# Normalised linear attention and channel mix on one core: batch 0's normalisation and token mix in fewer passes, and another written order

## The chip, the cores and the metric

The kernel runs on one core of a Trainium2 chip. The metric is the device time of one execution in microseconds (us); a time of the kernel is the median over several runs. The profile is one further execution, recorded by the hardware profiler. Its engines are TensorE (PE, with its weight loads as PEld), VectorE (DVE), ScalarE (ACT), GpSimd (POOL) and SyncE (SP). POOL and SP, and once ScalarE, also issue the transfers between the chip's main memory and the on-chip memory. Each engine executes its own instructions strictly in the order in which the program issued them; a wait at the head of an engine's queue holds all that stands behind it.

## The reference, cut to what matters

```python
# attention: q, k, v are [8 batches, 8 heads, 576 tokens, 64]
kv  = einsum('bhsd,bhse->bhde', k, v)
u   = einsum('bhsd,bhde->bhse', q, kv)
x   = u / sqrt(mean(u * u, axis=-1) + 1e-6) * g_norm      # then [batch, 576, 512]
# channel mix
x_prev = x shifted by one token within each batch (zeros first)
xk = mu_k * x + (1 - mu_k) * x_prev
xr = mu_r * x + (1 - mu_r) * x_prev
kk = maximum(xk @ w_k, 0)                # w_k is [512, 1024]
out = sigmoid(xr @ w_r) * ((kk * kk) @ w_v)
```

All inputs and the output are fp32; the kernel's matmuls take bf16.

## The kernel before

Attention goes by batch (0 to 7). For batches 0 and 1 the eight heads are handled as two halves z = 0 and 1; for the later ones both halves go together, which the names show as `.01`. The channel mix goes by groups g = 0 to 8 of 512 tokens, across batch borders, so group 2 takes tokens of batches 1 and 2, group 3 of batches 2 and 3.

Every step is a named piece: `add(name, engines, function, deps, bufs)`. The string `ORDER` lists all pieces, and `emit` (line 41) issues them in that order; `@A` or `@D` behind a name chooses ScalarE or VectorE. There is no planner at run time: the string alone fixes the order on each engine and on each transfer queue. The pieces of batch b, half z (and i for one half of the tokens):

- `ld.k`, `ld.v`, `ld.q`: loads with a cast to bf16, issued by POOL (lines 221 and 226); `ld.wk`, `ld.wv`, `ld.wr`: the weights (line 252). They go through one queue in the order of their issue. k, v and q have three buffers each. `ldh.k`, `ldh.v` are fp32 loads of batch 0's first half issued by SP (line 236), and `cst` casts them.
- `kv` (line 265) forms k times v in PSUM; `kc` copies it out, `ks` (line 271) rearranges it on TensorE, `kd` copies it again. `tq` (line 349) transposes q on VectorE. `u` (line 282) is q times kv, in PSUM.
- `uc` (line 368) takes u out of PSUM, scaled with g_norm, to the bf16 tile `uT`. `sq` (line 370) squares u on ScalarE. `ss` sums the squares over a head on TensorE (line 395 for batches 0 and 1, line 379 later). `rs` makes 1/rms on ScalarE (line 288). From batch 2 on, `sp` (line 417) spreads it with eight transfers of SP.
- `mul` (line 392) multiplies uT with 1/rms into `xT`. In `blends` (line 294), `d` is x minus x_prev; `mk` and `mr` scale d with mu - 1, two instructions each; `xk` and `xr` add x (line 313).
- The mix of group g: `k` (line 494, and 469 for group 0), `relu` (452), `ksq` (480 and 509), `r` (521), `sig` (531), `v` (541), `out` (554, and 568 for the last group), `st` for the stores (443).

`perm` and `ident` are two constant tables that POOL builds after VectorE has cleared them (`setp`); `cols` holds g_norm and mu - 1 as columns; `z:512` and `zz` are matmuls of zeros, which fill TensorE until data are there. `table` loads ScalarE's table for either 1/rms or the sigmoid when the other is loaded.

PSUM has four buffers `ps` for everything. In the order before, TensorE passes kv4.01 behind ss3 and two pieces ahead of the end of group 1's `v`.

Of the kernel before, what the change touches and what calls it, by code (L numbers as in the profile page):

```python
# [10 lines left out]
ALU = mybir.AluOpType  # L11
# [1 line left out]


ORDER = """
ldh.k ldh.v ld.q0.0 small table seta setp ident ld.v0.1 ld.k0.1 ld.q0.1 ld.q1.0 ld.v1.0 ld.k1.0 perm ld.wk0 ld.wk1 ld.k1.1 ld.v1.1 ld.wv0 ld.q1.1 ld.wv1 ld.wr ld.k2.01 ld.v2.01 ld.q2.01 zz cst.k0@A cst.k1@A cst.v1@D cst.v0@A z:512 z:512 z:512 z:512 z:512 z:512 z:512 z:512 z:512 z:512 z:512 z:512 z:512 z:512 z:512 z:512 kv0.0 setb tq0.0.1 kc0.0@A z:512 z:512 ks0.0 tq0.0.0 tr9 kd0.0@D z:512 z:512 z:512 u0.0.1 sq0.01 kv0.1 ld.v3.01 ld.k3.01 cols u0.0.0 sq0.00 uc0.01@D uc0.00@A kc0.1@D z:512 z:512 z:512 ss0.00 rs0.00 z:512 ss0.01 tq0.1.0 tq0.1.1 ld.q3.01 mul0.00 ks0.1 kd0.1@A d0.00 rs0.01 z:512 z:512 u0.1.0 uc0.10@A sq0.10 u0.1.1 uc0.11@A z:512 z:512 z:512 z:512 z:512 ss0.10 mul0.01 d0.01 mk0.00@D kv1.0 sq0.11 xk0.00 rs0.10 ss0.11 rs0.11 tq1.0.1 kc1.0@D ks1.0 tq1.0.0 kd1.0@A z:512 z:512 u1.0.0 mk0.01@D u1.0.1 sq1.00 xk0.01 k0.100 uc1.00@A uc1.01@A k0.000 sq1.01 mul0.10 d0.10 mk0.10@D xk0.10 mul0.11 d0.11 k0.010 mr0.11@A mk0.11@D xk0.11 k0.011 relu0.01 ss1.1 rs1.1 mr0.10@D xr0.10 k0.001 k0.101 relu0.00 mr0.00@D relu0.10 kv1.1 k0.110 ss1.0 ksq0.00 ksq0.10 k0.111 kc1.1@A v0.3.0 tq1.1.0 v0.2.0 tq1.1.1 ld.q4.01 ld.k4.01 ld.v4.01 rs1.0 relu0.11 ks1.1 kd1.1@D ksq0.11 mr0.01@A xr0.11 ksq0.01 xr0.00 v0.1.0 mul1.0 d1.0 u1.1.1 uc1.11@A u1.1.0 sq1.10 sq1.11 v0.0.0 xr0.01 v0.0.1 uc1.10@A v0.1.1 ss1.3 rs1.3 ss1.2 v0.3.1 rs1.2 mk1.0@D xk1.0 r0.0 mul1.1 d1.1 r0.1 sig0.0 r0.2 r0.3 sig0.1 v0.2.1 kv2.01 ld.v5.01 ld.k5.01 mk1.1@D xk1.1 out0.0 k1.2.0 k1.0.0 k1.1.0 out0.1 kc2.01@D ks2.01 tq2.01.1 tq2.01.0 k1.3.0 k1.2.1 k1.3.1 mr1.0@A kd2.01@A relu1.1 k1.0.1 u2.01.1 sq2.11 mr1.1@D k1.1.1 relu1.0 k1.6.0 k1.7.0 uc2.01@D uc2.11@D sq2.01 ksq1.1 u2.01.0 k1.6.1 k1.7.1 sq2.10 xr1.1 uc2.10@D k1.4.0 sq2.00 k1.5.0 uc2.00@D ss2 rs2 sp2.0 kv3.01 ld.v6.01 ld.q5.01 k1.4.1 k1.5.1 xr1.0 relu1.2 r1.0 kc3.01@D ksq1.0 ks3.01 kd3.01@A relu1.3 tq3.01.1 tq3.01.0 ld.q6.01 ld.k6.01 ksq1.2 r1.1 v1.0.0 ksq1.3 u3.01.0 uc3.10@D sig1.0 sq3.10 v1.1.0 v1.0.1 tq4.01.1 v1.1.1 uc3.00@D u3.01.1 tq4.01.0 sq3.00 uc3.11@A r1.2 r1.3 out1.0 sq3.11 v1.2.0 v1.3.0 sq3.01 ss3 mul2.0 sig1.1 kv4.01 ld.k7.01 ld.q7.01 ld.v7.01 sp2.1 rs3 kc4.01@A d2.0 v1.3.1 mk2.0@D xk2.0 st0.0 ks4.01 kd4.01@A v1.2.1 st0.3 uc3.01@A st0.2 mul2.1 d2.1 mk2.1@D xk2.1 u4.01.0 sq4.10 st0.1 uc4.10@A k2.2 uc4.00@A sq4.00 out1.1 st1.0 mr2.0@D k2.3 k2.0 k2.1 relu2.0 ksq2.0 relu2.1 ksq2.1 k2.4 k2.5 relu2.2 k2.6 k2.7 sp3.0 relu2.3 xr2.0 v2.3.0 mr2.1@D kv5.01 mul3.0 ksq2.2 u4.01.1 sq4.11 ksq2.3 sp3.1 d3.0 v2.2.0 st1.1 v2.2.1 uc4.11@A v2.1.0 uc4.01@A mul3.1 sq4.01 mr3.0@D ss4 xr3.0 kc5.01@A v2.1.1 v2.3.1 rs4 sp4.1 xr2.1 sp4.0 r2.2 v2.0.0 d3.1 mk3.1@A mr3.1@D xr3.1 xk3.1 tq5.01.0 ks5.01 kd5.01@A mk3.0@D xk3.0 v2.0.1 r2.3 sig2.1 out2.1 st2.3 r2.0 tq6.01.1 r2.1 sig2.0 out2.0 k3.2 k3.3 relu3.1 ksq3.1 k3.0 tq5.01.1 k3.4 k3.5 relu3.2 k3.1 mul4.1 d4.1 mr4.1@D relu3.0 ksq3.0 k3.6 k3.7 ksq3.2 u5.01.0 st2.0 st1.3 uc5.10@D relu3.3 ksq3.3 v3.3.0 uc5.00@A xr4.1 r3.0 mul4.0 sq5.10 tq6.01.0 r3.1 sq5.00 mk4.1@D sig3.0 r3.2 d4.0 mk4.0@D xk4.0 st2.1 r3.3 sig3.1 v3.3.1 kv6.01 kc6.01@A u5.01.1 uc5.11@D uc5.01@A sq5.11 tq7.01.1 v3.2.0 v3.2.1 ks6.01 kd6.01@D out3.1 v3.0.0 v3.0.1 st2.2 sq5.01 u6.01.1 xk4.1 ss5 rs5 sp5.0 v3.1.0 v3.1.1 mr4.0@D xr4.0 uc6.11@A st1.2 sq6.11 sq6.01 uc6.01@A tq7.01.0 k4.4 k4.5 k4.2 out3.0 st3.0 u6.01.0 relu4.2 uc6.10@D uc6.00@D sq6.10 k4.3 relu4.1 sq6.00 k4.0 k4.1 relu4.0 ksq4.1 k4.6 kv7.01 ss6 st3.2 ksq4.0 k4.7 r4.0 r4.1 kc7.01@D mul5.0 d5.0 relu4.3 ksq4.3 v4.1.0 sp5.1 mul5.1 rs6 st3.1 d5.1 ks7.01 kd7.01@D sp6.1 v4.2.0 ksq4.2 v4.3.0 sig4.0 u7.01.0 uc7.10@D v4.0.0 v4.2.1 v4.0.1 mk5.0@D mr5.1@A uc7.00@A sq7.00 r4.2 sq7.10 r4.3 mk5.1@D xk5.1 xr5.1 mr5.0@A sig4.1 mul6.1 xr5.0 xk5.0 d6.1 mk6.1@A sp6.0 mul6.0 v4.3.1 v4.1.1 out4.0 out4.1 st4.0 st4.2 k5.6 k5.7 relu5.3 ksq5.3 k5.2 k5.3 relu5.1 st4.3 ksq5.1 k5.0 k5.1 relu5.0 u7.01.1 sq7.01 sq7.11 d6.0 xk6.1 mk6.0@D uc7.11@D mr6.0@D k5.4 k5.5 st3.3 ksq5.0 r5.2 xr6.0 r5.3 st4.1 mr6.1@D ss7 uc7.01@A relu5.2 rs7 v5.1.0 sig5.1 ksq5.2 r5.0 sp7.0 r5.1 sig5.0 v5.0.0 v5.0.1 v5.1.1 xk6.0 k6.0 k6.1 relu6.0 xr6.1 r6.0 sp7.1 out5.0 st5.0 st5.1 v5.3.0 mul7.1 v5.2.0 k6.4 k6.5 relu6.2 ksq6.2 d7.1 ksq6.0 k6.2 k6.3 relu6.1 r6.1 mul7.0 r6.2 sig6.0 r6.3 k6.6 k6.7 v5.2.1 ksq6.1 v6.2.0 v6.3.0 d7.0 relu6.3 v6.1.0 mr7.0@A mk7.0@D xk7.0 v6.0.0 sig6.1 mr7.1@A mk7.1@D xk7.1 k7.4 k7.5 xr7.0 ksq6.3 v6.1.1 v6.0.1 out6.0 v6.3.1 v6.2.1 out6.1 st6.3 k8.2 k8.3 relu8.1 k7.2 v5.3.1 out5.1 k7.6 k7.7 k8.0 relu7.3 k7.3 relu7.1 ksq8.1 relu7.2 st6.0 st6.1 ksq7.3 st6.2 xr7.1 k7.0 k7.1 r7.0 relu7.0 r7.2 r7.1 r7.3 k8.1 k8.6 sig7.0 ksq7.2 ksq7.0 ksq7.1 k8.7 relu8.3 st5.3 relu8.0 r8.2 r8.3 st5.2 ksq8.0 v7.3.0 ksq8.3 v7.3.1 v7.1.0 v7.1.1 sig8.1 k8.4 k8.5 relu8.2 ksq8.2 v7.0.0 v7.0.1 v7.2.0 v7.2.1 sig7.1 out7.1 st7.2 st7.3 out7.0 v8.1.00 r8.0 r8.1 v8.2.00 v8.2.10 st7.0 v8.0.00 out8.20 sig8.0 st7.1 v8.1.10 st8.20 out8.10 v8.0.10 st8.10 v8.3.00 v8.3.10 out8.00 st8.00 out8.30 v8.3.01 v8.3.11 st8.30 out8.31 st8.31
"""


# [37 lines left out]
def kernel(  # L57
# [13 lines left out]
    nc = tc.nc  # L71
# [18 lines left out]
    X0 = 2  # L90
# [203 lines left out]
    def blends(b, z, name, x0, w, deps, mds, dd):  # L294
        xT = xTs[(NZ * b + z) % NX]
        cur, prev = slice(X0 + x0, X0 + x0 + w), slice(X0 - 1 + x0, X0 - 1 + x0 + w)
        cs, r0 = slice(x0, x0 + w), S * (b % RB) + x0

        def diff(_):
            nc.vector.tensor_tensor(out=get(dd)[:, :, cs], in0=xT[:, :, cur], in1=xT[:, :, prev], op=ALU.subtract)  # L300

        df = add("d" + name, "D", diff, deps=deps, bufs=[dd, x_buf[(b, z)]])
        done = {}
        for key, dst, m0 in (("k", xk, 0), ("r", xr, NHP)):
            md = mds[key]

            def mul(eng, md=md, m0=m0):
                for y in range(2):
                    hp = m0 + 2 * z + y
                    scale(eng, get(md)[:, y, cs], dd.t[:, y, cs], cols[:, hp:hp + 1])  # L310

            def plus(_, md=md, dst=dst):
                nc.vector.tensor_tensor(out=dst[:, 2 * z:2 * z + 2, r0:r0 + w], in0=md.t[:, :, cs], in1=xT[:, :, cur],  # L313
                                        op=ALU.add)

            m = add(f"m{key}" + name, "DA", mul, deps=[df, p_cols], bufs=[dd, md])
            done[key] = add(f"x{key}" + name, "D", plus, deps=[m] + x_free.get((b - RB, key), []),
                            bufs=[md, x_buf[(b, z)]])
        return done
# [3 lines left out]
    def attention(b):  # L323
# [40 lines left out]
        for z in range(NZ):  # L364
            for i, (c0, c1) in enumerate(PARTS):
                name, ps, w, cs = f"{b}.{z}{i}", us[z][i], c1 - c0, slice(c0, c1)
                uT, sq = bufs[z]["uT"], bufs[z]["sq"]
                uc = add("uc" + name, "DA", lambda eng, ps=ps, uT=uT, cs=cs, w=w: scale(
                    eng, get(uT)[:, :, cs], ps.t[:, :, 0:w], cols[:, 8:9]), deps=[pu[(z, i)], p_cols], bufs=[ps, uT])
                sq_ = add("sq" + name, "A", lambda _, ps=ps, sq=sq, cs=cs, w=w: nc.scalar.activation(  # L370
                    out=get(sq)[:, :, cs], in_=ps.t[:, :, 0:w], func=AF.Square), deps=[pu[(z, i)]], bufs=[ps, sq])
# [15 lines left out]
        for z in range(NZ):  # L387
            uT, sq, rs, dd = (bufs[z][t] for t in ("uT", "sq", "rs", "d"))
            xT, xb = xTs[(NZ * b + z) % NX], x_buf[(b, z)]

            def mul(_, cs, uT=uT, rs=rs, xT=xT):
                nc.vector.tensor_mul(out=xT[:, :, X0 + cs.start:X0 + cs.stop], in0=uT.t[:, :, cs], in1=rs.t[:, :, cs])  # L392

# [3 lines left out]
            if b == 0:  # L397
                muls = []
                for i, (c0, c1) in enumerate(PARTS):
                    ps, w, cs = Buf("ps"), c1 - c0, slice(c0, c1)  # L400
                    s = add(f"ss{b}.{z}{i}", "T", lambda _, ps=ps, c0=c0, w=w, sq=sq: [ones_mm(_, ps, y, c0, w, y, sq)
                            for y in range(2)], deps=[secs[(z, i)][1], p_setb], bufs=[ps, sq])
                    p = add(f"rs{b}.{z}{i}", "A", lambda _, ps=ps, w=w, cs=cs, rs=rs: rms(_, get(rs)[:, :, cs], ps.t[:, :, 0:w]),
                            deps=[s], bufs=[ps, rs])
                    muls = muls + [add(f"mul{b}.{z}{i}", "D", lambda _, cs=cs, mul=mul: mul(_, cs),
                                       deps=[p, secs[(z, i)][0], p_setb], bufs=[uT, rs, xb])]
                    done = blends(b, z, f"{b}.{z}{i}", c0, w, muls, mds[z], dd)
                    for key in "kr":
                        x_ready[b][key].append(done[key])
# [200 lines left out]
```

## Time and profile before

| what | value |
|---|---|
| time, median of 3 runs | 200.54 us (200.50 to 200.64) |
| time of the profiled execution | 200.29 us |
| its span, first to last instruction | 198.5 us |
| granted TensorE clock | 0.998 |
| TensorE busy | 189.4 us, 95% |
| VectorE busy | 136.1 us, 69% |
| ScalarE busy | 123.6 us, 62% |
| relu on ScalarE (line 452) | 36 times 1025 ns |
| matmuls of line 541 | 287 recorded, 66.4 us |
| loads by POOL's queue | 16.19 MB as written, in 11280 packets |
| transfers by SP's queue | 14.03 MB in 9588 packets |

How to read it: times inside the profile run from the first instruction. The lines of a group name the code line, the engine, the operation, the tile that is written and the tiles that are read, then the count, the busy time and the mean duration, and the idle time of that engine ahead of them with what ended it. A busy TensorE counts matmuls that overlap, so its share says how full the engine is, not how fast. The chain is the sequence of work that ended last, followed back from the last instruction to whatever released each step. In the views of the transfers, q0 is POOL's queue and q1 is SP's.

### The profile page before, as it was taken

What the parts mean: (1) busy time and instruction counts of PE and PEld (TensorE: products, weight loads), DVE (VectorE), ACT (ScalarE), POOL (GpSimd) and SP (SyncE); (2) the same over time, 40 slices, a digit from 0 to 9 for tenths busy, and PEclk for the clock granted to TensorE, in tenths of its full rate; (3) what the DMA queues carried; (4) which work ended last, traced back from release to release, by engine and by line L of the source; (5) the groups of instructions that cost most, each with busy time, mean ns of one, the idle gap of its engine ahead of it and who ended that gap; (6) DMA issues with size and microseconds to landing.
All of it is one profiled execution on the core that took longest, in us unless ns stands there. A gap on an engine that the chain in (4) does not pass through costs nothing.

```text
span 198.5 us, 4247 instructions
## 1 busy us (share of the span) xinstructions
PE 189.4 (95%) x1741; PEld 94.1 (47%) x1765; DVE 136.1 (69%) x242; ACT 123.6 (62%) x161; POOL 23.8 (12%) x42
## 2 busy tenths in 40 slices
PE   7998999998997999999999999999999999999992
PEld 2444864443544454444547744434444444444451
DVE  1579939999899378999986679896348246410631
ACT  3378995769897776848676697689255423652120
POOL 7843332220412100000000000000000000000000
PEclk9999999999999999999999999999999999999999
DMA  6999999999999999999706523242500017000064
GB/s 218 217 207 210 193 204 212 211 207 214 207 237 273 272 239 243 217 241 262 187 0 188 147 47 77 95 169 58 170 0 2 0 45 273 2 0 0 28 239 159
DMA packets 21031, 30.63 MB, mean 154 GB/s; under 512 B 1932, under 2 KB 14484, under 8 KB 21012
## 3 DMA queue, kind: packets, MB, share of 16 engines
q0 software_dynamic: 11280, 16.19, 45.6%
q1 hardware_dynamic: 9588, 14.03, 22.4%
q8 instruction: 14, 0.23, 0.5%
q10 hardware_dynamic: 144, 0.13, 0.2%
q14 instruction: 5, 0.04, 0.1%
HBM read 33.56 MB, written 9.44 MB: 217 GB/s over the span
## 4 chain that ended last, share of the span: by engine, by line
PE 66%; DMA 27%; POOL 3%; issue 1%; DVE 0%; POOLq 0%
PE ps L541 25%; PE ps L494 25%; DMA v<-in_v_dram 13%; PE ps L521 12%; DMA k<-in_k_dram 9%; DMA w_k<-in_moe_w_k_dram 6%; PE ps L282 2%; PE ps L265 1%; POOL k L226 1%; PE ps L379 1%; POOL v L226 1%; POOL q L221 1%; POOL perm L189 1%; PE ps L271 0%; DVE out L568 0%
## 5 line engine op out<-in xcount | busy, mean ns | idle before, releaser
L541 PE MATMUL ps<-w_v,sqk 128*128 128x512 bf16 (+1 forms) x287 | 66.4, 373 | 0.9 <-issue 0.5
L494 PE MATMUL ps<-xk,w_k 128*128 128x512 bf16 (+1 forms) x280 | 58.1, 355 | 0.6 <-issue 0.3
L452 ACT ACTIVATE relu<-ps 128x1024 bf16<-128x1024 f32 x36 | 36.1, 1025 | 35.6 <-PE ps L494 33.7
L541 PEld LDWEIGHTS <-sqk 128*128 128x128 bf16 x296 | 27.8, 98 | 32.1 <-issue 2.0
L494 PEld LDWEIGHTS <-w_k 128*128 128x128 bf16 x288 | 27.5, 98 | 27.3 <-issue 1.6
L509 DVE TENSOR_TENSOR sqk<-relu 128x1024 bf16<-128x1024 bf16 x32 | 21.7, 687 | 22.8 <-ACT relu L452 22.8
L521 PE MATMUL ps<-w_r,xr 128*128 128x512 bf16 x140 | 33.5, 379 | 0.3
L554 DVE TENSOR_TENSOR out<-ps,sig 128x1024 f32<-128x1024 f32 x16 | 19.2, 1218 | 12.4 <-PE ps L541 8.5
L531 ACT ACTIVATE sig<-ps 128x1024 bf16<-128x1024 f32 x18 | 18.3, 1022 | 9.2 <-PE ps L521 9.1
L370 ACT ACTIVATE sq<-ps 128x576 bf16<-128x576 f32 x32 | 20.0, 652 | 5.7 <-PE ps L282 4.1
L521 PEld LDWEIGHTS <-xr 128*128 128x128 bf16 x144 | 14.0, 98 | 16.5 <-issue 0.2
L136 DVE TENSOR_SCALAR md<-d,cols 128x576 bf16<-128x576 bf16 (+1 forms) x54 | 16.4, 347 | 0.3
L349 DVE STREAM_TRANSPOSE qT<-q 128x576 f32<-128x576 f32 (+1 forms) x20 | 14.9, 762 | 2.3 <-DMA q<-in_q_dram 2.1
L134 ACT ACTIVATE uT<-ps,cols 128x576 bf16<-128x576 f32 x19 | 13.7, 741 | 2.0 <-PE ps L282 1.9
L392 DVE TENSOR_TENSOR xT<-uT,rs 128x1152 bf16<-128x1152 bf16 (+1 forms) x18 | 12.4, 686 | 2.4 <-DMA rs<-rsc 2.3
L134 ACT ACTIVATE md<-d,cols 128x576 bf16<-128x576 bf16 (+1 forms) x18 | 12.0, 714 | 2.7 <-DVE d L300 2.7
L136 DVE TENSOR_SCALAR uT<-ps,cols 128x576 bf16<-128x576 f32 x13 | 10.4, 813 | 4.7 <-PE ps L282 3.2
L144 ACT ACT_TABLE_LOAD x10 | 12.8, 1283 | 0.9 <-PEq L594 0.7
L313 DVE TENSOR_TENSOR xr<-md,xT 128x1152 bf16<-128x1152 bf16 (+1 forms) x18 | 12.3, 687 | 0.7 <-ACT md L134 0.6
L313 DVE TENSOR_TENSOR xk<-md,xT 128x1152 bf16<-128x1152 bf16 (+1 forms) x18 | 12.4, 691 | 0.5
L300 DVE TENSOR_TENSOR d<-xT 128x1152 bf16<-128x1152 bf16 (+1 forms) x18 | 12.4, 691 | 0.4
L437 PE MATMUL ps<-zero 128*128 128x512 bf16 x32 | 10.8, 478 | 1.7 <-DVE ident L167 1.2
(49 smaller groups left out, 110.8 us busy)
## 6 DMA issues: line engine op xcount, KB each, us to landing
out_dram<-out SPq DMA_DIRECT2D x35, 256.0 KB, 3.1
k<-in_k_dram POOLq DMA_DIRECT2D x6, 576.0 KB, 24.8
v<-in_v_dram POOLq DMA_DIRECT2D x6, 576.0 KB, 25.4
q<-in_q_dram POOLq DMA_DIRECT2D x6, 576.0 KB, 25.1
rs<-rsc SPq DMA_DIRECT2D x48, 72.0 KB, 5.4
q<-in_q_dram POOLq DMA_DIRECT2D x4, 288.0 KB, 8.8
w_k<-in_moe_w_k_dram POOLq DMA_DIRECT2D x2, 512.0 KB, 12.5
w_v<-in_moe_w_v_dram POOLq DMA_DIRECT2D x2, 512.0 KB, 16.3
```

What stands on the lines that cost most here:

```text
L134: nc.scalar.mul(out=dst, in_=src, mul=col)
L136: nc.vector.tensor_scalar(out=dst, in0=src, scalar1=col, scalar2=None, op0=ALU.mult)
L313: nc.vector.tensor_tensor(out=dst[:, 2 * z:2 * z + 2, r0:r0 + w], in0=md.t[:, :, cs], in1=xT[:, :, cur], op=ALU.add)
L349: nc.vector.transpose(out=dst[part, js], in_=src[part, js])
L370: sq_ = add("sq" + name, "A", lambda _, ps=ps, sq=sq, cs=cs, w=w: nc.scalar.activation(out=get(sq)[:, :, cs], in_=ps.t[:, :, 0:w], func=AF ...
L452: nc.scalar.activation(out=get(rt), in_=ps.t, func=AF.Relu)
L494: nc.tensor.matmul(get(ps)[:, fc % 2, a0:a1], w_k_sb[:, cc, 128 * fc:128 * fc + 128], xk[:, cc, x0:x0 + a1 - a0], start=(cc == 0), stop=(c ...
L509: nc.vector.tensor_mul(out=get(sqk)[:, 2 * f2:2 * f2 + 2, :], in0=rt.t, in1=rt.t)
L521: nc.tensor.matmul(get(ps)[:, ci % 2, :], xr[:, cc, n0:n0 + 128], w_r_sb[:, cc, :], start=(cc == 0), stop=(cc == NHP - 1))
L531: nc.scalar.activation(out=get(sg), in_=ps.t, func=AF.Sigmoid)
L541: nc.tensor.matmul(get(ps)[:, bank, cs], sqk.t[:, fc, 128 * ci:128 * ci + 128], w_v_sb[:, fc, cs], start=(fc == 0), stop=(fc == NFC - 1))
L554: dv = add(f"out{g}.{c2}", "D", lambda _, ps=ps, sg=sg, ot=ot: nc.vector.tensor_mul(out=get(ot), in0=ps.t, in1=sg.t), deps=ms + [sg_done], ...
```

## The change

Three things are changed, in the code and in the order.

In batch 0 the pieces `uc` do not exist any more: `mul` takes u straight from PSUM and multiplies with g_norm and with 1/rms in one VectorE instruction. PSUM's buffer of u is therefore held until `mul` is through. In batch 0 also `mk` and `mr` do not exist: `xk` and `xr` are each two VectorE instructions that multiply d with the column of mu - 1 and add x. The other batches keep their code.

The string `ORDER` is a different one throughout. The order of the loads on POOL's queue is new: `perm` is built ahead of all of them, w_k's two parts follow directly behind batch 0's second half, and k and v of batch 5 come ahead of v, k and q of batch 4. On TensorE kv5.01 comes ahead of kv4.01. There are fewer zeros (29 words `z:512` for 34).

```diff
-ldh.k ldh.v ld.q0.0 small table seta setp ident ld.v0.1 ld.k0.1 ld.q0.1 ld.q1.0 ld.v1.0 ld.k1.0 perm ld.wk0 ld.wk1 ld.k1.1 ld.v1.1
- ld.wv0 ld.q1.1 ld.wv1 ld.wr ld.k2.01 ld.v2.01 ld.q2.01 zz cst.k0@A cst.k1@A cst.v1@D cst.v0@A
...
- kv0.0 setb tq0.0.1 kc0.0@A z:512 z:512 ks0.0 tq0.0.0 tr9 kd0.0@D z:512 z:512 z:512 u0.0.1 sq0.01 kv0.1 ld.v3.01 ld.k3.01 cols u0.0.0 sq0.00 uc0.01@D uc0.00@A kc0.1@D
...
- u3.01.1 tq4.01.0 sq3.00 uc3.11@A r1.2 r1.3 out1.0 sq3.11 v1.2.0 v1.3.0 sq3.01 ss3 mul2.0 sig1.1 kv4.01 ld.k7.01 ld.q7.01 ld.v7.01
...
+ldh.k ldh.v seta setp perm ld.q0.0 ld.q0.1 ld.v0.1 ld.k0.1 ld.wk0 ident ld.wk1 ld.v1.1 ld.k1.1 ld.q1.1 ld.wr ld.q1.0 ld.v1.0 ld.k1.0
+ ld.wv0 ld.wv1 ld.v2.01 ld.k2.01 ld.q2.01 table small zz cst.k0@D cst.k1@A setb cst.v0@A cst.v1@D tq0.0.1 tq0.0.0
...
+ kv0.0 tq0.1.0 kc0.0@A z:512 z:512 ks0.0 tr9 cols kd0.0@A u0.0.0 sq0.00 z:512 z:512 z:512 ss0.00 u0.0.1 rs0.00 mul0.00 d0.00 tq0.1.1 z:512 z:512
+ kv0.1 ld.k3.01 ld.v3.01 ld.q3.01 sq0.01 kc0.1@A ss0.01 rs0.01 ks0.1 kd0.1@A z:512 z:512 z:512 u0.1.0 sq0.10 xk0.00 z:512 z:512 z:512
+ ss0.10 mul0.01 d0.01 xk0.01 rs0.10 mul0.10 d0.10 u0.1.1 k0.000 sq0.11 ss0.11 rs0.11 k0.110 xk0.10 k0.100 mul0.11 k0.001 d0.11 xk0.11
...
+ mul1.1 kv1.0 ld.k5.01 ld.v5.01 kc1.0@D
...
+ kv2.01 ld.v4.01 ld.k4.01 ld.q4.01 xk1.1 kc2.01@A
...
+ u3.01.1 uc3.11@A uc3.10@D kv5.01 ld.k6.01 ld.v6.01 sq3.11 kc5.01@A v1.3.1 v1.1.0 ks5.01 kd5.01@A v1.1.1 uc3.01@A v1.0.0 sq3.01 ss3
+ v1.0.1 kv4.01 sp2.0 sp2.1 rs3 st0.0 mul2.0 d2.0 mk2.0@D xk2.0 mul2.1 d2.1 mk2.1@D st0.1 sp3.0 mr2.0@A xk2.1 k2.2
...
+            if b == 0:
+                def both(_, m0=m0, dst=dst):
+                    for y in range(2):
+                        hp = m0 + 2 * z + y
+                        nc.vector.scalar_tensor_tensor(out=dst[:, 2 * z + y, r0:r0 + w], in0=dd.t[:, y, cs], scalar=cols[:, hp:hp + 1],
+                                                       in1=xT[:, y, cur], op0=ALU.mult, op1=ALU.add)
+
+                done[key] = add(f"x{key}" + name, "D", both, deps=[df, p_cols], bufs=[dd, x_buf[(b, z)]])
+                continue
...
-                uc = add("uc" + name, "DA", lambda eng, ps=ps, uT=uT, cs=cs, w=w: scale(
+                uc = None if b == 0 else add("uc" + name, "DA", lambda eng, ps=ps, uT=uT, cs=cs, w=w: scale(
...
+            def mul_ps(_, cs, ps, rs=rs, xT=xT):
+                nc.vector.scalar_tensor_tensor(out=xT[:, :, X0 + cs.start:X0 + cs.stop], in0=ps.t[:, :, 0:cs.stop - cs.start],
+                                               scalar=cols[:, 8:9], in1=rs.t[:, :, cs], op0=ALU.mult, op1=ALU.mult)
...
-                    muls = muls + [add(f"mul{b}.{z}{i}", "D", lambda _, cs=cs, mul=mul: mul(_, cs),
-                                       deps=[p, secs[(z, i)][0], p_setb], bufs=[uT, rs, xb])]
+                    muls = muls + [add(f"mul{b}.{z}{i}", "D", lambda _, cs=cs, mul=mul_ps, pu_=us[z][i]: mul(_, cs, pu_),
+                                       deps=[p, pu[(z, i)], p_cols, p_setb], bufs=[us[z][i], rs, xb])]
```

## The prediction

> **What bounds the kernel now.** The page first: the span, the busy shares, and the chain that ended last.
>
> ```profile
> span 198.5 us, 4247 instructions
> PE 189.4 (95%) x1741; PEld 94.1 (47%) x1765; DVE 136.1 (69%) x242; ACT 123.6 (62%) x161; POOL 23.8 (12%) x42
> ...
> PE 66%; DMA 27%; POOL 3%; issue 1%; DVE 0%; POOLq 0%
> ```
>
> TensorE is the bound, and 27% of the chain are loads. The second view, the chain in order of time, says which and until when:
>
> ```profile
> 7.11 12.01 DMA w_k<-in_moe_w_k_dram
> 19.11 0.28 issue
> 19.40 17.53 DMA k<-in_k_dram
> 36.93 0.28 issue
> 37.22 24.95 DMA v<-in_v_dram
> 62.17 0.14 issue
> 62.30 0.77 PE ps L265 x72
> ```
>
> Up to 62.17 us the end hangs on the stream of loads: that piece is kv4.01, released by v4. From there to the last matmul (194.70) the chain is TensorE's alone. Third view, TensorE's waits between 60 and 64 us:
>
> ```profile
> PE ps L265 <- DMA v<-in_v_dram: 0.9, 1, 0.9
> ```
>
> So TensorE was ready for kv4.01 at 62.30 - 0.85 = 61.45 and lost 0.85 us. Any later start of kv4.01 moves the end one for one, less what was done before it. Fourth view, the DMA queues of the windows 54 to 58, 58 to 62 and 62 to 66 (packets, MB, share; q0 are the loads, q1 the spreads of 1/rms and the stores):
>
> ```profile
> q0 software_dynamic: 559, 0.63, 91.4%
> q1 hardware_dynamic: 320, 0.30, 27.9%
> ...
> q0 software_dynamic: 460, 0.51, 73.9%
> q1 hardware_dynamic: 427, 0.51, 43.5%
> ...
> q0 software_dynamic: 385, 0.43, 62.0%
> q1 hardware_dynamic: 383, 0.69, 51.7%
> ```
>
> Between 50 and 54, with q0 alone, 0.81 MB moved. The reader is to see that the stream is full, and that each MB on q1 takes about 0.6 MB from the loads: 0.83 - 0.6 x 0.30, 0.51 and 0.69 gives 0.65, 0.52 and 0.42.
>
> **The change, part by part.** The sum is made against the profiled execution, 200.29 us (span 198.5 and 1.8 around it); the median of the runs shown, 200.54, lies 0.25 above it.
>
> *Fused passes of batch 0.* Gone: four uT (one on VectorE at 0.82, three on ScalarE at 0.74) and eight scalings (six pairs on VectorE at about 0.5, two on ScalarE at 0.95): ScalarE loses 4.1 us of work. VectorE's mul, now out of PSUM, goes from 0.46 to about 0.82 (the PSUM row of uT, 813 ns). Eight adds of 0.46 become eight pairs of fused passes over 128x288. The trace shows none; the cheap end is a two-tensor bf16 pass (460 ns at 576, 757 at 1152, so 0.31 at 288), the dear end one element per cycle as from PSUM (692 ns at 512, 1218 at 1024, so 0.46). I take 0.46, nearer because a pass with scalar and second tensor does the work of both removed ones. VectorE: 0.8 + 1.8 + 3.0 + 3.7 = 9.3 us before, 3.3 + 7.4 = 10.7 after (8.3 at the cheap end). It lies on the first chunk's chain and, through xk, in front of TensorE until about 27 us.
>
> *First chunk.* kv0.0 stays at 7.56, behind the same 17 zero matmuls. kd0.0 on ScalarE (done 9.6) lets u0.0.0 start when the transposes end, 9.85 for 10.19. Square 0.65, ss0.00 at 11.0; rs0.00 0.74, done 12.25; mul 0.82, d 0.46, a transpose 0.72 queued in front, xk0.00 0.92: ready at 15.2 (16.87 before). TensorE is later: kv0.1 needs v0.1 and k0.1, now third and fourth load (10.4 and 11.8 by the landings of the third and fourth load before) and a PSUM buffer that rs0.00 frees at 12.25; kc, ks, kd, u0.1.0, a square, ss0.10 and u0.1.1 follow, each by its row: k0.000 at 16.5, 3.1 before the old 19.66. w_k's first half, fifth load for eighth, lands near 14.5 (19.11 before), so it no longer holds.
>
> *Until kv2.01.* Of the 3.1 us, 2.0 is work only put behind (kv1 and ks1 of one half, its u, ss0.11: 0.7 + 0.35 + 0.7 + 0.25). New waits in TensorE's order: ss0.11 on its square 0.35, u1.1.1 on transposes behind xr0.11, xr0.00 and ksq0.00 0.5, ks1.0 on a copy behind mul1.1 0.55, u1.0.1 on transposes 0.3: 1.7, where before lost 0.7. Lead: 3.1 - 2.0 - 1.0 = 0.1: kv2.01 at about 40.3 (40.38 before). Ends: 39.7, when its own k2 lands (19.4 + 17.5 = 36.9 and one landing on, v2's 39.7), and 41.5.
>
> *Order of loads and of kv.* The new order loads k5 and v5 ahead of v4, k4 and q4, and puts kv5.01 ahead of kv4.01. kv4.01 needs k4, which is now the 25th load on POOL's queue; before it needed v4, the 24th. Bytes through the 25th: ten halves of 0.295, five weights of 0.524, ten of 0.590: 11.47 MB. Loads are equal in number and bytes up to the 23rd, so their landings are those of before. The 25th of before (v5, issued at 41.48, 26.2 to landing) came at 67.7 beside q1's traffic. After, SP sends sp2 (0.59 MB) and two stores (0.52 MB) and then waits for rs3; before, it sent four or five stores. q0 had moved 11.15 MB by 62; at 0.21 MB per us less 0.6 of the 0.32 MB left on q1, the missing 0.32 MB takes 2.5 us: 64.5. Landing is noted later than the bytes: k4 before, 10.29 MB, moved by about 55.8 and landed at 57.7; v4 60.0 and 62.2. With 2.0: k4 lands at 66.5.
>
> *perm first.* perm (1.1 us on POOL, behind setp's memset that ends at 1.45) now precedes all loads of POOL: first issue at 2.6 for 1.24, 1.4 later for every load of that queue. Rows: the first q0 packet starts near 4.9, 3.7 after its issue, just as the staged loads run out (1.05 of 1.18 MB by 4.9). If it waited for those, the shift is 0; if 3.7 us is its own latency, 1.3. The Trainium skill ("DMA: Bandwidth & Descriptors", Latency and other measured facts) gives about 1 us from issue to first byte on this path; by that the shift would be 0 and the sum 0.4 lower; the trace shows 3.7 and cannot say which. I take 0.4, nearer the first end because the hand-over falls together with the end of the staged loads. k4: 66.9; kv4.01 at 67.0.
>
> *Other edits.* rs and sig alternate more: 12 table loads for 10, 2 x 1.28 us on ScalarE, hidden (ScalarE idles 35.6 us in front of relu alone). Five zero matmuls fewer, off the path. Engines of uc, kc, kd, mk, mr of batches 1 to 7: a few tenths either way in waits that TensorE does not see (VectorE is idle 22.8 us in front of ksq). SP's stores are reordered; the last five pieces of TensorE, the last store and so the last 3.8 us stay.
>
> *The sum.* TensorE reaches kv4.01 at 61.45 + 2.66 (v1.3.1 and v1.2.1 1.73, kv5 0.71, ks5 0.22, now ahead of it) = 64.1, with the gaps of 0.2 about 64.3. It waits until 67.0, 2.7 us. Behind it in its queue stand k2.2 and everything after, though xk2.1 is ready near 65. The rest is 194.70 - 62.30 - 2.66 = 129.7: last matmul 196.8, span 200.6, time 202.4, on the median's footing 202.6.
>
> **The rivals.**
> (1) *Not slower: k4 lands before TensorE comes.* For: fewer stores on q1. Against: the ledger above, and k4's turn in the queue. It decides when kv4.01 starts before 62.30 + 2.66 = 64.96, that is when the 25th load is 2.0 us earlier. With no wait at all, 64.3 + 129.7: 194.0, 0.7 less: 199.9; with a front lead of 1 us, 198.9.
> (2) *A change that shows nothing:* front hidden, k4's wait about 0.7: within 0.4 of 200.5. Against: 1.3 to 2 us of landing would have to go.
> (3) *The full shift of 1.3 and a clock that falls.* k4 at 67.8, wait 3.6: 203.5. In this trace the first 13 zeros come every 0.43 us until 6.3 and then every 0.22; no later wait is above 0.85. Should the clock fall in the wait, some 3.4 us at half pace cost 1.7: 205.2. The Trainium skill ("TensorE: Matmul & The Clock Gate", Part 1) says that about 3.4 us of idleness halve the clock; by it my 2.7 us do not, 3.6 do; no wait here tests it.
> (4) *A second stall after kv4.01*, in VectorE's order: tq6.01.0, d3, mk3, xk3 end near 86.5 and k3.6 is due at 87.3. If VectorE is 2 us late, 1.2 more: 203.8.
>
> **How the numbers follow.** Likeliest, the wait of 2.7 us: 60%, 201.4 to 203.8 (shift 0 to 1.3, landing lag 1.8 to 2.2). (1) 17%, (2) 7%, (3) 8%, (4) 8%. Range 199.9 to 204.4: it leaves out half of (1), the cold clock of (3) and the upper part of (4), some 16%. Within 0.2% (0.4 us) is what measurement can't tell from no change: faster 17%, same 7%, slower 76%.
>
> **What would show it.** Chain of after: k<-in_k_dram ending near 67 and then L265, where v<-in_v_dram ended at 62.17. TensorE's waits: L265 behind k<-in_k_dram of 2 to 4 us; none for w_k. L469 begins at 16 to 17 us. The fused passes at 288 near 460 ns, the PSUM mul near 820. Wrong if L265's wait is under 1 us, if q0 has moved 11.5 MB before 63 us, or if TensorE has more than 1 us of waits after 70.

## The result, and the profile after

| kernel | median | executions | lowest to highest |
|---|---|---|---|
| before | 200.40 us | 9 | 199.91 to 200.71 |
| after | 201.51 us | 9 | 201.14 to 203.22 |

The ratio is 1.0074, with a 95% interval of 1.0045 to 1.0103: the change costs 0.7%. The medians alone differ by 1.11 us, 0.55%; the ratio also counts the two executions of after above 203 us. The profiled execution of after took 201.43 us, 0.08 below the median, with a span of 199.6 us.

The page of after gives the span, the busy shares, and further down the shares of the chain that ended last.

```profile
span 199.6 us, 4250 instructions
...
PE 190.3 (95%) x1760; PEld 93.1 (47%) x1760; DVE 137.9 (69%) x235; ACT 122.0 (61%) x158; POOL 23.6 (12%) x42
...
PE 76%; DMA 16%; ACT 2%; POOL 2%; issue 1%; DVE 1%; POOLq 0%; ACTq 0%
```

The loads' share of the chain has fallen from 27% to 16%, and yet the span is 1.1 us longer. A share says nothing of where a load ends. The chain in order of time says it (start, duration, what):

```profile
41.26 0.73 POOL v L226
41.99 23.98 DMA k<-in_k_dram
65.97 0.04 issue
66.02 0.78 PE ps L265 x72
66.79 2.70 PE ps L507 x12
```

This is k4, issued at 41.99 and landed at 65.97, and kv4.01 behind it. Before, the last load on the chain ended at 62.17. From 66.02 to the last matmul the chain is TensorE's alone; the few ScalarE steps of the page lie before 28 us. TensorE's waits from 64 us to the end (line waited at, releaser, us in total, times, longest):

```profile
PE ps L265 <- DMA k<-in_k_dram: 1.7, 1, 1.7
```

It is the only one. TensorE's timeline (start, duration, instruction, idle time ahead of it) shows the places that the prediction set times for:

```profile
16.52 1.05 PE L482 MATMUL ps<-xk,w_k 128*128 128x256 bf16 x8
...
40.15 0.78 PE L265 MATMUL ps<-v,k 64*64 64x64 bf16 x72
...
58.39 0.77 PE L265 MATMUL ps<-v,k 64*64 64x64 bf16 x72 [0.32 <-DMA v<-in_v_dram]
...
66.02 0.78 PE L265 MATMUL ps<-v,k 64*64 64x64 bf16 x72 [1.74 <-DMA k<-in_k_dram]
```

They are k0.000, kv2.01, kv5.01 and kv4.01. Without its wait kv4.01 would have begun at 66.02 - 1.74 = 64.28. The last matmul ends at 195.72, 129.70 us after kv4.01 began; in before the last matmul ended at 194.70.

The queues in the windows 54 to 58, 58 to 62 and 62 to 66 of after (packets, MB, share; q0 the loads, q1 SP's transfers):

```profile
q0 software_dynamic: 475, 0.53, 77.0%
q1 hardware_dynamic: 446, 0.42, 40.1%
...
q0 software_dynamic: 483, 0.54, 78.2%
q1 hardware_dynamic: 359, 0.48, 39.4%
...
q0 software_dynamic: 438, 0.73, 98.9%
q1 hardware_dynamic: 117, 0.21, 16.2%
```

In the third window SP sends only 0.21 MB, and the loads get 0.73 MB for the 0.43 of before: where q1 is quiet, the loads move more.

### The profile page after: what moved, and what is told of

Read it like the earlier page. It is cut to its first block, busy times and chain, and to the rows that moved or that the text cites. A ratio compares the mean times of both kernels' runs of the same rounds, so it can differ in the third digit from the quotient of the medians.

```text
span 199.6 us, 4250 instructions
## 1 busy us (share of the span) xinstructions
PE 190.3 (95%) x1760; PEld 93.1 (47%) x1760; DVE 137.9 (69%) x235; ACT 122.0 (61%) x158; POOL 23.6 (12%) x42
## 4 chain that ended last, share of the span: by engine, by line
PE 76%; DMA 16%; ACT 2%; POOL 2%; issue 1%; DVE 1%; POOLq 0%; ACTq 0%
PE ps L554 28%; PE ps L507 24%; DMA k<-in_k_dram 16%; PE ps L534 13%; PE ps L482 3%; PE ps L265 3%; PE ps L282 2%; ACT relu L465 1%; PE ps L408 1%; PE ps L450 1%; PE ps L388 1%; PE ps L271 1%; POOL v L226 1%; POOL q L221 1%; ACT sq L379 1%
## 5 line engine op out<-in xcount | busy, mean ns | idle before, releaser
L554 PE MATMUL ps<-w_v,sqk 128*128 128x512 bf16 (+1 forms) x296 | 67.2, 374 | 0.0
L507 PE MATMUL ps<-xk,w_k 128*128 128x512 bf16 (+1 forms) x288 | 58.8, 356 | 0.5 <-issue 0.5
L534 PE MATMUL ps<-w_r,xr 128*128 128x512 bf16 x144 | 34.0, 379 | 0.0
L136 DVE TENSOR_SCALAR md<-d,cols 128x576 bf16<-128x576 bf16 x44 | 14.0, 370 | 0.4
L134 ACT ACTIVATE uT<-ps,cols 128x576 bf16<-128x576 f32 x15 | 10.9, 742 | 2.9 <-PE ps L282 2.9
L313 DVE TENSOR_TENSOR xr<-md,xT 128x1152 bf16<-128x1152 bf16 x14 | 10.4, 751 | 1.6 <-ACT md L134 1.4
L405 DVE TENSOR_TENSOR xT<-uT,rs 128x1152 bf16<-128x1152 bf16 x14 | 10.4, 750 | 1.1 <-ACT rs L288 0.6
L313 DVE TENSOR_TENSOR xk<-md,xT 128x1152 bf16<-128x1152 bf16 x14 | 10.4, 754 | 0.6 <-ACT md L134 0.4
L450 PE MATMUL ps<-zero 128*128 128x512 bf16 x30 | 9.4, 454 | 1.2 <-DVE zero L164 1.2
L265 PE MATMUL ps<-v,k 64*64 64x64 bf16 x576 | 7.7, 194 | 2.4 <-DMA k<-in_k_dram 2.1
```

The costliest lines, as they stand in the source:

```text
L136: nc.vector.tensor_scalar(out=dst, in0=src, scalar1=col, scalar2=None, op0=ALU.mult)
L507: nc.tensor.matmul(get(ps)[:, fc % 2, a0:a1], w_k_sb[:, cc, 128 * fc:128 * fc + 128], xk[:, cc, x0:x0 + a1 - a0], start=(cc == 0), stop=(c ...
L534: nc.tensor.matmul(get(ps)[:, ci % 2, :], xr[:, cc, n0:n0 + 128], w_r_sb[:, cc, :], start=(cc == 0), stop=(cc == NHP - 1))
L554: nc.tensor.matmul(get(ps)[:, bank, cs], sqk.t[:, fc, 128 * ci:128 * ci + 128], w_v_sb[:, fc, cs], start=(fc == 0), stop=(fc == NFC - 1))
```

## The experiments

Where a diff shows a line of `ORDER`, it is an excerpt: only the words around the edit. Line numbers are each kernel's own.

### The wait taken away: kv4.01 three pieces later (e1)

The loads and all work stay; kv4.01 is put behind k2.2, k2.3 and k2.0 on TensorE, with the three pieces that depend on it.

```diff
- ss3 v1.0.1 kv4.01 sp2.0 sp2.1 rs3
+ ss3 v1.0.1 sp2.0 sp2.1 rs3
...
- k2.2 sp3.1 out1.0 k2.3 kc4.01@A out1.1 st1.3 k2.0 ks4.01 relu2.1 kd4.01@A
+ k2.2 sp3.1 out1.0 k2.3 out1.1 st1.3 k2.0 kv4.01 relu2.1 kc4.01@A
...
- ld.q7.01 k2.4 k2.5
+ ld.q7.01 k2.4 ks4.01 kd4.01@A k2.5
```

> The kernel after with kv4.01 moved three pieces back on TensorE, behind k2.2, k2.3 and k2.0; the loads stay as they are. Theory (kv4.01 stands at the head of TensorE's queue and waits for k4's load): k2.2 starts when xk2.1 is ready, 64.5 us, kv4.01 comes at about 67.2 with k4 long landed at 66.0, the wait of 1.74 us goes, and with 0.25 us left in front of k2.2 the last matmul ends near 194.2 instead of 195.7: 199.9 to 200.1 us, ratio to the kernel before 0.998. Rival (the fused passes cost the time) and rival (the loss sits elsewhere in the new order): no change, 201.4 to 201.6, or the wait turns up again behind kv4.01.

Measured: 199.86 us (199.43 to 200.23), ratio to before 0.9976 (0.9965 to 0.9987): faster than both kernels. TensorE's timeline of e1:

```profile
64.05 2.83 PE L507 MATMUL ps<-xk,w_k 128*128 128x512 bf16 x12
66.81 0.78 PE L265 MATMUL ps<-v,k 64*64 64x64 bf16 x72
```

The reader is to see that the 2.8 us of group 2's matmuls, which in after stand behind kv4.01, now fill the time until k4 is there; kv4.01 has no idle time ahead of it. (The first two matmuls of k2.2 read only xk2.0; the third starts at 64.56, when xk2.1 is ready.) The gain over after by the medians, 201.51 - 199.86 = 1.65 us, is close to the 1.74 us of the wait. So the wait alone carries more than the whole loss of after (1.1 us).

### The fused passes: undone in after, undone in e1, done alone in before (e2, e7, e3)

In e2 (from after) and e7 (from e1) batch 0 has its `uc` on ScalarE again, behind each square, and its `mk` and `mr` on VectorE, each directly ahead of what reads it. The code of batch 0's `mul`, `xk` and `xr` is that of before again (not all of it is shown).

```diff
- u0.0.0 sq0.00 z:512
+ u0.0.0 sq0.00 uc0.00@A z:512
...
- mul0.01 d0.01 xk0.01
+ mul0.01 d0.01 mk0.01@D xk0.01
...
-                uc = None if b == 0 else add("uc" + name, "DA", lambda eng, ps=ps, uT=uT, cs=cs, w=w: scale(
+                uc = add("uc" + name, "DA", lambda eng, ps=ps, uT=uT, cs=cs, w=w: scale(
```

> The new order with batch 0's passes apart again as before (uT by ScalarE behind each square, mk and mr by VectorE in front of xk and xr). Theory: VectorE's time hardly changes (mul 0.46 for 0.82, scaling and add 0.95 for 0.95), ScalarE has 3 us more; k0 starts 0 to 0.5 us later and TensorE reaches kv4.01 0 to 1 us later, but kv4.01 still starts at 66.0 with its load: 201.3 to 201.7. Rival (the fused passes, or PSUM held longer by them, cost the time): it falls to about 200.4.

Measured for e2: 201.60 us (201.36 to 203.56), ratio to before 1.0077 (1.0047 to 1.0107), that of after. Its k0.000 starts at 16.96 and its kv2.01 at 40.65, 0.4 to 0.5 us later than in after, and then:

```profile
66.05 0.78 PE L265 MATMUL ps<-v,k 64*64 64x64 bf16 x72 [1.86 <-DMA k<-in_k_dram]
```

The load sets the start of kv4.01, so a later front changes nothing. TensorE had even made the delay good by then: it reaches kv4.01 at 64.19, for 64.28 in after, since at kv5.01 (58.30) it waits for nothing where after waited 0.32 us for v5. e7 asks whether the passes are worth something once that wait is gone.

> The kernel with kv4.01 put back behind k2.0, and batch 0's passes apart again. With the wait for k4's load gone TensorE is full from k0 on, so the front now counts: with the passes apart k0 started 0.4 us later in the trace (16.96 for 16.52) and kv2.01 0.5 later (40.65 for 40.15). Theory: 0.3 to 0.5 us more than with kv4.01 put back and the passes together, 200.2 to 200.4. If the passes are worth nothing on TensorE's path: 199.9.

Measured for e7: 200.00 us (199.62 to 200.87), ratio 0.9975 (0.9961 to 0.9989). This missed: none of the expected 0.3 to 0.5 us is seen, though the two intervals, about 0.25 us to either side, could hide some of it. In both kernels TensorE still meets a load at kv5.01; the timeline of e1 and then of e7:

```profile
58.33 0.77 PE L265 MATMUL ps<-v,k 64*64 64x64 bf16 x72 [0.23 <-DMA v<-in_v_dram]
```

```profile
58.31 0.77 PE L265 MATMUL ps<-v,k 64*64 64x64 bf16 x72 [0.33 <-DMA v<-in_v_dram]
```

v5's landing starts both at 58.3. But in these two traces little was left for it to hide. The difference of the front is 0.55 us at k0.000 (16.79 for 16.24), 0.09 us at kv2.01 (40.33 for 40.24), and e7 reaches kv5.01 first, at 57.98 for 58.10.

In e3 the order is that of before, and only the token mix of batch 0 is fused (its eight `mk0` and `mr0` words leave `ORDER`; the code is that of the first hunk of the diff).

```diff
- mul0.01 d0.01 mk0.00@D kv1.0
+ mul0.01 d0.01 kv1.0
...
- d0.11 k0.010 mr0.11@A mk0.11@D xk0.11
+ d0.11 k0.010 xk0.11
```

> The kernel before, its order untouched, with the token mix of batch 0 alone in one pass (mk and mr of batch 0 gone; uT stays). Theory: a pair of fused passes takes 0.95 us, as scaling and add together did; two scalings leave ScalarE; kv4.01 still waits for v4 at 62.2: 200.2 to 200.6, ratio 1.000. Rival (the fused passes cost the time): over 200.9.

Measured: 200.68 us (200.41 to 202.06), ratio 1.0029 (1.0010 to 1.0047): slightly slower, where no difference was expected. In that order two of the scalings were on ScalarE, and there VectorE takes them over: a fused pair is 0.95 us where the add alone was 0.46. That this is the cause was not shown: the profiled execution was at the top of its range, 202.05 us, with its first piece of attention at 8.60 us for 7.56, and can't be compared step by step. The pass out of PSUM alone wasn't tried in the old order.

### The order of the loads (e4, e9, e5)

All three start from after and exchange k4, v4 and k5, v5 among the loads. In e4 batch 4 also takes the place of batch 5 on TensorE, and kv5.01 goes behind u4.01.1; the copies and `ks` of both batches move with them (not all of that is shown).

```diff
- kv1.0 ld.k5.01 ld.v5.01 kc1.0@D
+ kv1.0 ld.k4.01 ld.v4.01 kc1.0@D
...
- kv2.01 ld.v4.01 ld.k4.01 ld.q4.01
+ kv2.01 ld.v5.01 ld.k5.01 ld.q4.01
...
- uc3.10@D kv5.01 ld.k6.01 ld.v6.01 sq3.11 kc5.01@A v1.3.1 v1.1.0 ks5.01 kd5.01@A
+ uc3.10@D kv4.01 ld.k6.01 ld.v6.01 sq3.11 kc4.01@A v1.3.1 v1.1.0 ks4.01 kd4.01@A
...
- ss3 v1.0.1 kv4.01 sp2.0
+ ss3 v1.0.1 sp2.0
...
- u4.01.1 ksq2.3
+ u4.01.1 kv5.01 ksq2.3
```

> The kernel after with batch 4 ahead of batch 5 again: k4, v4 are loaded where k5, v5 were and kv4.01 stands where kv5.01 stood; kv5.01 goes behind u4.01.1. Theory: kv4.01 comes at about 58.4 behind its load (23rd in the queue, 58.2), kv5.01 near 76 waits for nothing, TensorE passes 64.3 without a stop: 199.6 to 199.9, the same as with kv4.01 put back, or a little better since k2.2 has 0.25 us of slack from v1 pieces no more. Rivals: no change, 201.4 to 201.6.

Measured: 201.89 us (201.55 to 202.49), ratio 1.0079 (1.0062 to 1.0096). A miss. TensorE's waits of e4 between 54 and 82 us:

```profile
PE ps L265 <- ACT sq L379: 1.4, 1, 1.4
PE ps L534 <- ACT kv L128: 0.5, 1, 0.5
PE ps L265 <- DMA v<-in_v_dram: 0.3, 1, 0.3
```

The wait for k4 is gone; only v4 is waited for, 0.3 us at 58.58. In its place kv5.01, at 77.19, waits 1.4 us for a PSUM buffer that a square on ScalarE still reads, and group 2's r then 0.5 for the buffer of kv5.01 itself. Those 1.9 us are the size of the wait taken away, and they were made by where I put kv5.01, behind the two u that fill the buffers. e9 moves kv5.01 on, to behind k3.5, and leaves the rest of e4.

```diff
- u4.01.1 kv5.01 ksq2.3
+ u4.01.1 ksq2.3
...
- k3.5 relu3.2 ksq3.2 k3.2 k3.3 relu3.1
+ k3.5 kv5.01 relu3.2 kc5.01@A ksq3.2 k3.2 k3.3 ks5.01 relu3.1 kd5.01@A
```

> Batch 4 ahead of batch 5 in loads and on TensorE, as in the run of that kind before, but kv5.01 behind k3.5 and not behind u4.01.1, where it waited 1.37 us for one of the four PSUM buffers that u4 holds, and r2.0 another 0.46 for its copy. Theory: nothing waits at kv4.01 beyond 0.3, kv5.01 finds its load and a buffer: 199.6 to 200.0, as with kv4.01 put back. Rival (the order of the loads is not what costs): 201.4 to 201.9.

Measured: 200.22 us (199.60 to 200.56), ratio 0.9985 (0.9971 to 0.9999), a little over the range expected; neither kv waits (58.74 and 87.07). Six of its twelve executions, the profiled one among them, had a granted clock of 0.991 and took 200.31 to 200.56 us; the other six took 199.60 to 200.13. In the profiled one the clock is at half from 11.69 to 15.10 us, long before kv4.01. The loss of after is gone by this way too: batch 4 has both its loads and its kv early, and no kv stands at the head of TensorE's queue ahead of its load.

e5 goes the other way: it exchanges the loads alone, so that TensorE meets kv5.01 first while k5 is now the 25th load.

> The kernel after with the loads of k4, v4 and of k5, v5 exchanged and nothing else: kv5.01 still stands ahead of kv4.01 on TensorE. Theory (each load lands at its turn in the queue, and TensorE's first kv behind the 25th load starts there): kv5.01, which starts at 58.4 in the kernel after, now waits for the 25th load, to 66.0, so 7.6 to 7.9 us; kv4.01 follows 5.6 us later without a wait, and the end moves by about 5.6: 206.5 to 207.5 us. Rival (the order of loads and kv is not what sets the end): below 203.

Measured: one execution, 210.28 us, span 208.5. TensorE's timeline, and the clock by stretches (stretch, length, busy time and count of PE, PEld, DVE, ACT and POOL, granted clock, DMA share, GB/s):

```profile
66.30 1.18 PE L265 MATMUL ps<-v,k 64*64 64x64 bf16 x72 [8.43 <-DMA k<-in_k_dram]
```

```profile
60.00:62.00 2.00, 0.00 (x0) 0.00 (x0) 1.97 (x4) 0.00 (x0) 0.00 (x0) 0.99 1.15 282
62.00:64.00 2.00, 0.00 (x0) 0.00 (x0) 1.90 (x5) 0.00 (x0) 0.00 (x0) 0.50 1.18 248
...
66.00:68.00 2.00, 1.70 (x74) 1.33 (x75) 0.00 (x0) 0.37 (x1) 0.22 (x1) 0.50 1.05 212
70.00:72.00 2.00, 2.00 (x9) 0.98 (x8) 0.00 (x0) 0.53 (x2) 0.00 (x0) 0.50 1.15 203
72.00:74.00 2.00, 2.00 (x16) 0.77 (x15) 0.00 (x0) 1.98 (x3) 0.00 (x0) 0.95 1.21 207
```

The 25th load lands at nearly the same time (66.25 for 65.97) whichever batch it carries, and whoever reads it first pays. The time above what was expected, some 3 us, is the clock: it is at half from 61.98 to 72.22, and kv5.01 and all up to 72.22, 5.9 us, run at half pace, which costs 3.0 us.

### The next wait, looked for (e8, e10)

e8 takes e1 and also puts kv5.01 behind v1.3.1, past its 0.23 us for v5.

```diff
- uc3.10@D kv5.01 ld.k6.01 ld.v6.01 sq3.11 kc5.01@A v1.3.1 v1.1.0 ks5.01 kd5.01@A v1.1.1
+ uc3.10@D sq3.11 v1.3.1 kv5.01 ld.k6.01 ld.v6.01 kc5.01@A v1.1.0 v1.1.1 ks5.01 kd5.01@A
```

> The kernel with kv4.01 put back, and kv5.01 one piece back too, behind v1.3.1. kv5.01 waits 0.3 to 0.5 us for v5's load (58.25). Theory: v1.3.1 runs in that gap, 199.4 to 199.6. Rival (the wait turns up again, at ks5.01 or ss3): 199.9.

Measured: 200.14 us (199.79 to 201.50), ratio 0.9991 (0.9975 to 1.0008): above the range expected, and no gain over e1. TensorE's waits between 56 and 70 us:

```profile
PE ps L388 <- ACT sq L379: 0.5, 1, 0.5
```

The wait for v5 is gone, and ss3 waits for its square instead. On ScalarE the two copies of batch 5 stand ahead of that square in e1 too, but with kv5.01 later they come about 1 us later (the second at 62.33 for 61.20). e10 makes the same move in before: kv4.01, which waited 0.85 us there, goes behind v1.3.1.

```diff
- mul2.0 sig1.1 kv4.01 ld.k7.01 ld.q7.01 ld.v7.01 sp2.1 rs3 kc4.01@A d2.0 v1.3.1 mk2.0@D
+ mul2.0 sig1.1 sp2.1 rs3 d2.0 v1.3.1 kv4.01 ld.k7.01 ld.q7.01 ld.v7.01 kc4.01@A mk2.0@D
...
- st0.0 ks4.01 kd4.01@A v1.2.1 st0.3
+ st0.0 v1.2.1 ks4.01 kd4.01@A st0.3
```

> The kernel before with kv4.01 alone put back, behind v1.3.1 (its copies and ks4 behind v1.2.1). There TensorE waited 0.85 us for v4. Theory: v1.3.1 runs in that wait, kv4.01 starts near 62.4 with its load landed, k2.2 at 64.7 instead of 65.4 (xk2.1 is ready at 64.6): 0.7 us less, 199.6 to 199.8, ratio 0.996 to 0.997. Rival (another wait follows at u4.01.0 or k2.2): 200.3.

Measured: 200.47 us as the median of nine executions (200.21 to 200.70), ratio 1.0011 (1.0001 to 1.0020): no gain. Two further executions, of 205.23 and 208.74 us at granted clocks of 0.989 and 0.975, are not in these numbers; no trace was taken of them. TensorE's waits between 58 and 68 us:

```profile
PE ps L282 <- ACT kv L128: 0.5, 1, 0.5
PE ps L494 <- ACT uT L134: 0.2, 1, 0.2
```

kv4.01 starts at 62.39 without waiting, but u4.01.0 behind it now waits for ScalarE's copy of kv, and the gain is spent. So before could not be mended by that step, where after could: in after, group 2's first twelve matmuls are ready to fill the gap, and nothing soon behind kv4.01 needs it.

### The table perm, behind the first loads again (e6, e11)

From after; `perm` goes behind the fourth load, so that POOL issues its first load at 1.24 us for 2.32.

```diff
- seta setp perm ld.q0.0 ld.q0.1 ld.v0.1 ld.k0.1 ld.wk0
+ seta setp ld.q0.0 ld.q0.1 ld.v0.1 ld.k0.1 perm ld.wk0
```

> The kernel after with perm behind the first four loads on POOL's queue, so that the first load is issued near 1.2 us and not at 2.3. Theory (the first packets wait for the staged loads of SP, which fill the engines until about 5): the first q lands at 7.5 to 8.3 as before, k4 at 65.5 to 66.5, 201.2 to 201.8. Rival (3 to 4 us of latency from issue to first packet): every load comes 1.1 us earlier, k4 at 64.9, 200.4.

Measured: one execution, 203.04 us. The first load lands at 7.29 for 7.93 and w_k's first half at 13.97 for 14.69; by the seventh and eighth load the lead is gone (18.76 and 20.97 for 18.96 and 20.88), and k4 lands at 65.90 for 65.97. In between the loads land up to 0.4 us earlier than in after (v5 at 57.84 for 58.25), which is no more than executions with the same front differ by (v5 at 57.93 in e2, 58.45 in e4). That execution is 1.6 us above after for another reason, shown below. e11 is the same kernel over several executions.

> The same kernel as the one with perm behind the first four loads, timed in rounds, since that single execution ran at a granted clock of 0.988. There the first loads landed 0.6 to 0.7 us earlier, k0 began at 15.81 for 16.52, and k4 landed at 65.90 for 65.97. Theory: the front's 0.7 us only lengthens the wait at kv4.01: 201.3 to 201.6, as the kernel after. Rival (the front sets the end): 200.7 to 200.9.

Measured: 202.52 us (201.39 to 203.29, four executions), ratio 1.0095 (1.0059 to 1.0131), above what was expected. TensorE's timeline of e6, and the clock by stretches:

```profile
65.95 0.78 PE L265 MATMUL ps<-v,k 64*64 64x64 bf16 x72 [2.08 <-DMA k<-in_k_dram]
...
66.66 4.40 PE L507 MATMUL ps<-xk,w_k 128*128 128x512 bf16 x12
```

```profile
66.00:67.00 1.00, 1.00 (x73) 0.74 (x74) 0.57 (x1) 0.08 (x1) 0.00 (x0) 0.80 1.04 212
67.00:68.00 1.00, 1.00 (x4) 0.39 (x3) 0.00 (x0) 0.29 (x1) 0.00 (x0) 0.50 1.07 217
...
70.00:71.00 1.00, 1.00 (x7) 0.49 (x6) 0.00 (x0) 0.71 (x1) 0.00 (x0) 1.00 1.09 233
```

The front is 0.3 to 0.7 us earlier, k4 is not, so the wait grows from 1.74 to 2.08 us; and behind the longer wait the clock is at half for 3.41 us, from 66.59 to 70.00. The same twelve matmuls that take 2.77 us in after take 4.40. In e11's profile it is the same: a wait of 2.11 us, and half the clock from 67.02 for 3.41 us. Of the five executions of this kernel three took 203.0 to 203.3 us, of after's nine two; the intervals of the two ratios overlap, so that the earlier front makes the kernel slower is not shown. It gained nothing.

## Why the prediction was right, step by step

The mechanism was the predicted one, and e1 shows it by taking the wait away with the loads and the work unchanged: kv4.01 stands at the head of TensorE's queue for k4, the 25th load.

- *TensorE's arrival at kv4.01*: 64.3 predicted, 64.28 measured. On the way, k0.000 at 16.52 (16.5), kv2.01 at 40.15 (40.3), xk2.1 ready at 64.49 (near 65). The sum has no wait at kv5.01, where 0.32 us went to v5, so that the arrival fits to 0.02 us is partly luck.
- *The rest behind kv4.01*: 129.7 predicted, 129.70 measured. Behind it the view lists no other wait of TensorE, so rival (4), a stall near k3.6, did not come, and the other edits' zero holds, twelve table loads among them.
- *The landing of k4* is the term that was mis-sized: 66.9 predicted, 65.97 measured, so a wait of 1.74 us for 2.7, and 201.43 for 202.4. Between the medians the loss is 1.1 us where 2.1 were forecast, about half. Two parts make up the 0.9 us. The shift by perm was taken as 0.4; e6 gives 0.07 at k4. The first packet of POOL's queue starts at 5.20 in after and at 4.98 in e6, although it was issued 1.08 us earlier there (1.4 were assumed), so the lower end was nearly right. The Trainium skill ("DMA: Bandwidth & Descriptors", Latency and other measured facts), with its 1 us to the first byte, gave that end. The other part is the landing behind the bytes, 1.5 us and not 2.0. The loads up to k4 are 11.47 MB, and this is what q0 had moved by 64.5 us in after:

```profile
q0 software_dynamic: 8537, 11.46, 100.8%
```

  The 64.5 was predicted, but by two errors that cancel: q0 had moved 11.07 MB by 62 (11.15 assumed), and q1 then carried 0.21 MB for the 0.32 assumed. In before the 25th load landed 2.7 us behind the same bytes (11.47 MB at 65.0, landed at 67.7), so the lag is no constant. The likeliest case reached down to 201.4, further than the two terms named for it: no shift and a lag of 1.8 give 201.8. That 201.51 fell inside is owed to that margin.
- *The signs named ahead*: the wait of 2 to 4 us and k4's landing near 67 were missed (1.74 and 65.97). The others were met, and none of the three that would have made the prediction wrong appeared.
- *The fused passes*: 0.46 us each predicted at 288 columns, 0.47 measured as half of a pair, and the PSUM pass 0.82 as predicted. The times of VectorE in the first chunk:

```profile
11.85 0.82 DVE L401 SCALAR_TENSOR_TENSOR xT<-ps,cols,rs 128x576 bf16<-128x576 f32 x1 [1.40 <-ACT rs L288]
...
14.00 0.94 DVE L320 SCALAR_TENSOR_TENSOR xk<-d,cols,xT 128x288 bf16<-128x288 bf16 x2
```

  That they would be worth nothing at the end was right, and e2 and e7 show it. The prediction named the cover only loosely; in e2 it is the loads, v5 at 58.3 and k4 at 66.0. In e7 the later front had shrunk to 0.1 us by kv2.01, and the runs do not show where.
- *Rival (1)* priced the case without a wait at 199.9; e1 has 199.86.
- *Rival (3)*: the price of a falling clock, 1.7 us, was right, and the condition was wrong. I held that 2.7 us would not do it; 2.08 did in e6. In after itself two of the nine executions took 203.07 and 203.22 us, with granted clocks of 0.989 and 0.987 where the profiled one had 1.000: that is 1.6 to 1.8 us more, the price of one such stretch. No trace of those two was taken, so that they are the same event is inferred.

## What to carry to other kernels

When a load binds, count which load in its queue each consumer needs and set that landing against the consumer's arrival; work gained upstream only lengthens the wait. Before making the front faster, look for pieces behind the waiting instruction that are ready and can go ahead of it: three pieces moved (e1) turned a loss of 0.7% into a gain of 0.24%. Then read what the moved piece held and what reads it soon: in e4, e8 and e10 the wait came back at a PSUM buffer or behind ScalarE's work.

## What the runs showed of the hardware that was not expected

The granted clock fell behind short waits. Waits of 2.08 and 2.11 us (e6, e11) were followed by 3.41 us at half the clock; the profiled waits of 1.74 and 1.86 us (after, e2) were not. In e5 the wait began near 57.9, the clock fell at 61.98 and stayed down for 10.24 us, three times 3.41, beyond the wait's end. The falls of one trace also lie whole multiples of 3.413 us apart: in e6 and in e11 the next fall, behind the last work, comes 39 such steps after the one at the wait (66.59 to 199.71, and 67.02 to 200.14). The Trainium skill ("TensorE: Matmul & The Clock Gate", Part 1) describes a free-running activity window of 3,413 ns; the lengths agree with it. The same page of the Trainium skill (section "Why this matters for your kernels") asks for no idle gaps above about 3 us between bursts of matmuls; here staying below 3 us was not enough.

How long TensorE was busy in the window ahead of a fall does not settle it. The stretches of one window each, of e6, e11, after and e9 (same columns as for e5):

```profile
63.18:66.59 3.41, 1.33 (x76) 0.74 (x73) 3.35 (x4) 2.59 (x4) 0.22 (x1) 1.00 1.15 217
63.61:67.02 3.41, 1.30 (x76) 0.80 (x75) 2.74 (x3) 2.25 (x4) 0.01 (x1) 1.00 1.14 219
62.99:66.40 3.41, 1.67 (x60) 0.70 (x55) 3.38 (x5) 3.19 (x4) 0.59 (x1) 1.00 1.15 219
8.28:11.69 3.41, 2.15 (x26) 1.08 (x23) 2.44 (x5) 1.11 (x3) 1.38 (x3) 1.00 1.14 193
11.69:15.10 3.41, 3.41 (x52) 1.69 (x44) 2.63 (x5) 1.93 (x4) 1.17 (x2) 0.50 1.13 211
```

The clock fell behind 1.33 us of work in e6 and 1.30 in e11. In after it fell at 199.52 at the end; 40 steps back from there a window runs from 62.99 to 66.40, wholly around the wait, and behind its 1.67 us of work the clock stayed up. A limit between those would fit, were it not for e9: there the clock fell at 11.69, behind 2.15 us of work. What else about the work counts is open, and so is which execution falls: one of e11's four took 201.39 us at a clock of 1.000. The place of the window alone does not explain the two long executions of after, since in its trace the window already had the whole wait in it.

Also, an earlier first issue brought the first loads 0.6 to 0.7 us forward, but k4, the 25th load, by only 0.07 us.
